# Moving two pieces of work in a fused attention and feed-forward kernel: half of the first output weights ahead of one batch's values, and one batch's row sums into consecutive units

## The chip, the cores and the metric

The kernel runs on one core of a Trainium2 chip. The metric is the device time of one execution in microseconds (us), as a median over several executions. A profile is one execution recorded by the hardware profiler. Its "span" is about 2 us shorter than the time.

The engines are called PE (tensor engine, matmuls), PEld (its weight loads), DVE (VectorE), ACT (ScalarE), POOL (GpSimd) and SP (the engine whose queue issues most transfers here). A "q" behind a name means its sequencer, for example SPq.

## The reference, cut to what matters

```python
# 8 batches, 8 heads, 576 rows, head dimension 64
kv  = einsum('bhsd,bhse->bhde', k, v)          # "states", one 64x64 matrix for each head
o   = einsum('bhsd,bhde->bhse', q, kv)
o   = o / sqrt(mean(o*o, -1) + 1e-6) * g_norm  # row sums of squares are needed here
x   = o.transpose(0, 2, 1, 3).reshape(4608, 512)
xn  = x / sqrt(mean(x*x, -1) + 1e-6) * rms_g
out = (silu(xn @ w_gate) * (xn @ w_val)) @ w_out    # 512 -> 1536 -> 512
```

The inputs and the output are float32. The kernel casts to bf16 for the matmuls.

## The kernel before

It works in nine stages. Stage n runs the feed-forward part for batch n's first 512 rows: twelve "up" units of 8 matmuls each (gate and value, 128 columns of d_ff), then "down" products. Between these units it works on the attention of batch n+1, so that the next stage's input `xnt` is ready in time. The ninth stage does the 64 rows left of every batch.

Stage 0 is special: while it runs, the weights and the inputs of batches 1 and 2 are still coming in. Here are the parts that the change touches.

```python
    # order of loads on SP's queue
    alloc_kv(1, "k"); load_kv(1, "k", nc.sync)
    alloc_kv(1, "v"); load_kv(1, "v", nc.sync)
    load_wo(0)                    # output weights, block 0: two loads of 512 KB
    load_q(1); load_wo(1); load_wo(2); load_batch(2)
    ...
    for j in range(4, NF):        # stage 0's up units 4 to 11
        ffn.up(j)
        ...
        if j == 9:
            for i in range(3): cast_kv(1, "k", i, DVE)
        if j == 10:
            cast_kv(1, "k", 3, DVE)
            for i, engine in enumerate((SC, DVE, GP, DVE)): cast_kv(1, "v", i, engine)
    for i, engine in enumerate((SC, GP, DVE, SC)): round_wo(0, i, 1, engine)
    ...
    att1.kv_products((0, 1, 2, 3))          # states of batch 1: 72 small matmuls
    att1.kv_copy()                          # ACT, then DVE
    clear_tail_rows(1, DVE)                 # two memsets
    for i, engine in enumerate((DVE, SC, DVE, SC)):
        cast_q(1, slice(2 * i, 2 * i + 2), engine)
    for c in range(4):
        down_part(c, 0, 4)                  # 16 down matmuls
    turns.q_turn(0, SC)                     # query transposes on PE; need all four casts
    turns.q_turn(1, DVE)
    for blk in (1, 2):
        for i in range(4): round_wo(blk, i, 1, GP)
    for c in range(2): down_part(c, 4, 6)   # needs the first half of block 1
```

In the later stages a table of steps says after which unit each piece of the next batch's attention runs. `a.o(c)` makes 128 rows of attention output. `a.sums(c)` is a multiplication and a reduction on VectorE. `a.head`, `a.guess` and `a.root` turn the sums into row scales, `a.scale` applies them, and `a.x_rows` transposes the rows by DMA into the next stage's `xnt`.

```python
            kv0, os = (2, (4, 5, 7, 8)) if n == 1 else (0, (2, 3, 5, 6))
            for c, u in enumerate(os):
                steps[u].append(lambda a=a, c=c: a.o(c))
                steps[u + 1].append(lambda a=a, c=c: a.sums(c))
            late = 2 * int(n == 1)
            steps[8 + late] += [a.head]
            steps[9 + late] += [a.guess, a.root]
            ...                             # scale and x_rows in unit 11
```

Of the kernel before, what the change touches and what calls it, by code (L numbers as in the profile page):

```python
# [20 lines left out]
def kernel(  # L21
# [12 lines left out]
    nc = tc.nc  # L34

    B, H, S, D = q.shape
    d_model = H * D
# [40 lines left out]
    PE, DVE, SC, GP = nc.tensor, nc.vector, nc.scalar, nc.gpsimd  # L78
# [20 lines left out]
    wo_view = moe_w_out.rearrange("(c p) d -> p c d", p=128)  # L99

    def stage(n=2048):
        return stage_pool.tile([128, MAIN * T + MAIN], FP32, name="st")[:, 0:n]

    def cast(engine, dst, src):
        if engine is SC:
            engine.copy(out=dst, in_=src)  # L106
        else:
            engine.tensor_copy(out=dst, in_=src)
# [7 lines left out]
    def alloc_kv(b, name):  # L116
        raws[b, name] = stage(MAIN * T + MAIN)

    def pairs_raw(b, name):
        return raws[b, name][:, 0 : NS * C * D].rearrange("p (j x) -> p j x", j=NS)  # L120

    def pairs_buf(b, name):
        flat = bufs[b][name].rearrange("p t h d -> p (t h d)")
        return flat[:, 0 : NS * C * D].rearrange("p (j c d) -> p j c d", j=NS, c=C)

    def load_kv(b, name, queue, js=slice(0, NS)):
        src = srcs[name][b]
        if b < EARLY:
            view = src.rearrange("h s d -> (h s d)").rearrange("(j p x) -> p j x", j=NS, p=128)
            queue.dma_start(out=pairs_raw(b, name)[:, js, :], in_=view[:, js, :])  # L130
            return
        raw = raws[b, name]
        queue.dma_start(
            out=raw[:, 0 : MAIN * T].rearrange("p (h x) -> p h x", h=H),
            in_=src[:, 0:MAIN, :].rearrange("h (p t) d -> p h (t d)", t=T),
        )
        queue.dma_start(
            out=raw[0:TAIL, MAIN * T :].rearrange("r (h d) -> r h d", h=H),
            in_=src[:, MAIN:S, :].rearrange("h r d -> r h d"),
        )  # L140
# [3 lines left out]
    def cast_kv(b, name, i, engine):  # L144

        if b < EARLY:
            cast(engine, pairs_buf(b, name)[:, i].rearrange("p c d -> p (c d)"), pairs_raw(b, name)[:, i, :])
        elif i < NS:
            hs = slice(2 * i, 2 * i + 2)
            src = raws[b, name][:, 0 : MAIN * T].rearrange("p (h t d) -> p t h d", h=H, t=T)  # L150
            cast(engine, bufs[b][name][:, 0:T, hs, :], src[:, :, hs, :])
        else:
            src = raws[b, name][0:TAIL, MAIN * T :].rearrange("r (h d) -> r h d", h=H)
            cast(engine, bufs[b][name][0:TAIL, T], src)

    def load_q(b):
        st = stage()
        raws[b, "q"] = st
        for hs in (slice(0, 4), slice(4, 8)) if b < EARLY else (slice(0, H),):
            nc.sync.dma_start(  # L160
                out=st.rearrange("p (h x) -> p h x", h=H)[:, hs],
                in_=q[b, hs, 0:MAIN, :].rearrange("h (p t) d -> p h (t d)", t=T),
            )
# [4 lines left out]
    def cast_q(b, hs, engine):  # L168
        src = raws[b, "q"].rearrange("p (h t d) -> p t h d", h=H, t=T)[:, :, hs, :]
        cast(engine, bufs[b]["q"][:, :, hs, :], src)  # L170
# [9 lines left out]
    w_st = {}  # L180
# [24 lines left out]
                out=dst, in0=src, scalar1=rowscale[:, s : s + 1], scalar2=1.0, op0=OP.mult, op1=OP.mult  # L205
            )

    def load_wo(blk):
        st = stage()
        ap = st.rearrange("p (c d) -> p c d", d=d_model)  # L210
        for i in (0, 2):
            nc.sync.dma_start(out=ap[:, i : i + 2, :], in_=wo_view[:, 4 * blk + i : 4 * blk + i + 2, :])
        w_st["o", blk] = ap

    def round_wo(blk, i, n, engine):
        c = 4 * blk + i
        cast(engine, wo_sb[:, c : c + n, :], w_st["o", blk][:, i : i + n, :])
# [60 lines left out]
    def clear_tail_rows(i, engine):  # L278

        for t in (kbs[i], vbs[i]):  # L280
            engine.memset(t[TAIL:128, T], 0.0)
# [306 lines left out]
    for j in (2, 3):  # L588
# [4 lines left out]
        out=gam[NS : NS + 1, :].rearrange("o (i d) -> o i d", i=2),  # L593
        in_=g_norm.rearrange("(o d) -> o d", o=1).unsqueeze(1).to_broadcast([1, 2, D]),
# [54 lines left out]
    def state0(j, dummies):  # L649
        ps = att_pool.tile([128, 512], FP32, name="att_ps")  # L650
        warm(ps, max(dummies, 1), 512 if dummies else 128)
        kv_pair(ps[:, 0:128], 0, j, True, True)
        return ps
# [35 lines left out]
    for j in (0, 1):  # L689
        cast_kv(0, "k", j, DVE)  # L690
        cast_kv(0, "v", j, SC)
    kv0 = state0(0, 0)
# [26 lines left out]
        out=gsq, in0=gcol, scalar=1.0 / d_model, in1=gcol, op0=OP.mult, op1=OP.mult  # L719
# [63 lines left out]
            load_w(blk, name, nc.sync)  # L783
    alloc_kv(1, "k")
    load_kv(1, "k", nc.sync)
    alloc_kv(1, "v")
    load_kv(1, "v", nc.sync)
    load_wo(0)
    load_q(1)
    load_wo(1)  # L790
    load_wo(2)
# [44 lines left out]
    for j in range(4, NF):  # L836
        ffn.up(j)
        for s in {4: (0, 1), 5: (2,), 6: (3,)}.get(j, ()):
            round_w(4, "g", s, SC)
        if j == 6:  # L840
            for s in (0, 1):
                round_w(4, "v", s, DVE)
        if j == 7:
            clear_tail_rows(0, DVE)
        if j == 9:
            for i in range(3):
                cast_kv(1, "k", i, DVE)
        if j == 10:
            cast_kv(1, "k", 3, DVE)
            for i, engine in enumerate((SC, DVE, GP, DVE)):  # L850
                cast_kv(1, "v", i, engine)
    for i, engine in enumerate((SC, GP, DVE, SC)):
        round_wo(0, i, 1, engine)
    alloc_xnt(1)

    def f_cols(j):
# [19 lines left out]
    def down_part(c, lo, hi):  # L876
        ffn.down_products(c, lo, hi, pools[c])

    def round_wo_halves(blk):
        round_wo(blk, 0, 2, DVE)  # L880
        round_wo(blk, 2, 2, SC)

    att1.kv_products((0, 1, 2, 3))
    att1.kv_copy()
    clear_tail_rows(1, DVE)
    for i, engine in enumerate((DVE, SC, DVE, SC)):
        cast_q(1, slice(2 * i, 2 * i + 2), engine)
    for c in range(4):
        down_part(c, 0, 4)
    turns.q_turn(0, SC)  # L890
    turns.q_turn(1, DVE)
    for blk in (1, 2):
# [65 lines left out]
    for n in range(1, B + 1):  # L958
        ffn = Ffn(n)
        steps = {u: [] for u in range(NF + T)}  # L960
        if n + 2 < B:
            steps[2].append(lambda n=n: load_batch(n + 2))
        if n == B - 3:
            load_q_tails()
        if n == 1:
            steps[0] += [lambda i=i: cast_kv(2, "k", i, DVE) for i in (2, 3)]
            steps[0] += [lambda i=i: cast_kv(2, "v", i, SC) for i in (0, 1)]
            steps[1] += [lambda i=i: cast_kv(2, "v", i, SC) for i in (2, 3)]
            steps[0] += [lambda name=name: cast_kv(2, name, NS, GP) for name in ("k", "v")]
        if n < B:  # L970
            a = atts[n + 1]
            kv0, os = (2, (4, 5, 7, 8)) if n == 1 else (0, (2, 3, 5, 6))
            if not a.tail:
                steps[kv0] += [lambda a=a: a.kv_products((0, 1))]
                steps[kv0 + 1] += [lambda a=a: a.kv_products((2, 3)), a.kv_copy]
# [6 lines that stand above are left out]
            for c in range(T):  # L982
                steps[10 if c == 0 and not late else 11] += [lambda a=a, c=c: a.scale(c), lambda a=a, c=c: a.x_rows(c)]
        b = n + 2
        if b < B:
            steps[10] += [lambda b=b: alloc_q(b)]
            for i in range(2):
                steps[11] += [lambda b=b, i=i: cast_q(b, slice(4 * i, 4 * i + 4), SC)]
            for i in KV_CASTS:
                steps[12 + i // 3] += [lambda b=b, i=i: cast_kv(b, "k", i, SC)]  # L990
                steps[14 + i // 3] += [lambda b=b, i=i: cast_kv(b, "v", i, SC)]
            for c in range(T):
                steps[13].append(lambda b=b, c=c: atts[b].q_rows(c))
        if b == B:
            for i in range(2):
                steps[11] += [lambda i=i: cast_q_tails(2 * i, 2, SC)]
            for c in range(T):
                steps[13].append(lambda c=c: turn_q_tails(c))
        for unit in range(NF + T):
            if unit < NF:  # L1000
                ffn.up(unit)
            elif n == B and unit == NF + T - 1:
                ffn.down_last(unit - NF)
            else:
                ffn.down(unit - NF)
            for step in steps[unit]:
                step()
# [30 lines left out]
```

## Time and profile before

| | |
|---|---|
| time, median of the first 3 executions | 325.81 us (325.27 to 326.08) |
| span of the profile | 323.0 us |
| PE busy | 315.8 us, 98% |

The first part of the profile page gives the busy time of each engine, its share of the span and its number of instructions. The fourth part gives the shares of the chain that ended last. Here are the two lines of the kernel before.

```profile
PE 315.8 (98%) x1927; PEld 157.1 (49%) x1927; DVE 180.6 (56%) x373; ACT 179.3 (56%) x320; POOL 18.1 (6%) x40
...
PE 88%; DVE 5%; DMA 3%; SPq 2%; issue 1%; ACT 1%; DVEq 0%
```

PE is the bound, so a change can only win where PE stands still. The waits view (who waited for whom: us in total, times, longest) names two of these places in the part that the change touches.

```profile
PE g_ps L473 <- DMA xnt<-xna: 0.5, 1, 0.5
PE att_ps L266 <- DVE vb L108: 0.2, 1, 0.2
```

The second one in the timeline (start, length, engine, line, operation, tiles, count, and in brackets the idle time before): PE runs 18 of batch 1's state products, then stands until VectorE has cast a piece of v. From one start to the next, less the usual pitch, the hole is 0.36 us.

```profile
39.36 0.47 PE L266 MATMUL att_ps<-vb,kb 64*64 64x64 bf16 x18
39.52 0.81 DVE L108 CAST vb<-st 128x576 bf16<-128x576 f32 x2
40.02 1.04 PE L266 MATMUL att_ps<-vb,kb 64*64 64x64 bf16 x54 [0.19 <-DVE vb L108]
```

The first one is at the start of stage 2. In the chain of waits (start, length, what), the last transposed input lands at 89.40 us and PE follows.

```profile
86.80 2.60 DMA xnt<-xna
89.40 0.14 issue
89.54 1.02 PE g_ps L473 x4
```

The last down matmul of stage 1 starts at 88.68 us and takes 0.216 us of PE's pitch. The hole up to 89.54 us is therefore 0.65 us. VectorE's timeline shows where the lateness comes from: the last reduction (L362) ends at 77.86 us, so the `h` product of unit 10 (the second line) and all that follows it are late. The scaling (L379), which feeds the transposes, starts at 81.68 us.

```profile
76.64 1.22 DVE L362 TENSOR_REDUCE ssq<-sq 128x16 f32<-128x1024 bf16 x1
77.78 0.68 DVE L479 TENSOR_TENSOR h_sb<-silu,v_ps 128x512 bf16<-128x512 bf16 x1
78.37 0.17 DVE L366 TENSOR_SCALAR u<-ssq 128x32 f32<-128x32 f32 x1
...
81.68 2.50 DVE L379 TENSOR_TENSOR xna<-outa,s1y 128x512 bf16<-128x512 bf16 x4
```

### The profile page before, as it was taken

To read this page: it belongs to the slowest core of one execution; us is meant where nothing else is said; L and a number is where in the kernel's file an instruction comes from. 1 tells how busy PE (TensorE), PEld (TensorE's weight loads), DVE (VectorE), ACT (ScalarE), POOL (GpSimd) and SP (SyncE) were. 2 spreads that over 40 slices of the span, in tenths; PEclk is the share of its full clock that TensorE was granted. 3 is DMA by queue.
4 is the path that set the end of the run, shared out by engine and by line. 5 is a ranking of instruction groups with operands and counts; after the bars stand their busy time and mean duration, and the time that the engine had idled before them with its cause. 6 is when DMAs were issued, how large, how long until landed. Compare 5 with 4: busy or idle time off the path is not lost.

```text
span 323.0 us, 5146 instructions
## 1 busy us (share of the span) xinstructions
PE 315.8 (98%) x1927; PEld 157.1 (49%) x1927; DVE 180.6 (56%) x373; ACT 179.3 (56%) x320; POOL 18.1 (6%) x40
## 2 busy tenths in 40 slices
PE   8899999999999999999999999999999999999995
PEld 3584455544455445444544455445544444444443
DVE  4785858478437932794279416850696068703310
ACT  3687557666757476647674766576554355233321
POOL 1263241100000000000000000000000000000000
PEclk9999999999999999999999999999999999999999
DMA  7999999996369457934791378946002600240014
GB/s 273 350 349 387 378 373 291 223 282 158 66 196 294 130 137 171 287 91 106 198 335 45 72 202 200 313 79 177 34 2 49 179 34 1 48 148 3 0 35 97
DMA packets 74437, 54.87 MB, mean 170 GB/s; under 512 B 42280, under 2 KB 67116, under 8 KB 74412
## 3 DMA queue, kind: packets, MB, share of 16 engines
q1 hardware_dynamic: 74044, 53.89, 58.2%
q10 hardware_dynamic: 368, 0.66, 0.6%
q8 instruction: 15, 0.25, 0.3%
q14 instruction: 10, 0.08, 0.1%
HBM read 37.75 MB, written 9.44 MB: 146 GB/s over the span
## 4 chain that ended last, share of the span: by engine, by line
PE 88%; DVE 5%; DMA 3%; SPq 2%; issue 1%; ACT 1%; DVEq 0%
PE g_ps L473 27%; PE v_ps L473 26%; PE o_ps L515 23%; PE att_ps L273 2%; DMA st<-in_v_dram 2%; PE att_ps L344 2%; DVE h_sb L479 1%; PE v_ps L490 1%; DMA xnt<-xna 1%; PE v_ps L515 1%; PE g_ps L515 1%; DVE xna L379 1%; DMA out_dram<-o_sb 1%; SPq L386 1%; PE att_ps L266 1%
## 5 line engine op out<-in xcount | busy, mean ns | idle before, releaser
L479 DVE TENSOR_TENSOR h_sb<-silu,v_ps 128x512 bf16<-128x512 bf16 x104 | 70.9, 683 | 110.8 <-ACT silu L478 61.8
L473 PE MATMUL g_ps<-xnt,wg_sb 128*128 128x512 bf16 x416 | 106.8, 379 | 0.5 <-DMA xnt<-xna 0.5
L473 PE MATMUL v_ps<-xnt,wv_sb 128*128 128x512 bf16 x416 | 106.8, 379 | 0.0
L478 ACT ACTIVATE silu<-g_ps 128x512 bf16<-128x512 f32 x104 | 62.4, 601 | 63.9 <-PE g_ps L473 53.7
L515 PE MATMUL o_ps<-wo_sb,h_sb 128*128 128x512 bf16 x396 | 87.4, 379 | 0.0
L473 PEld LDWEIGHTS <-wv_sb 128*128 128x128 bf16 x416 | 40.6, 98 | 49.2 <-DVE wv_sb L204 0.5
L515 PEld LDWEIGHTS <-h_sb 128*128 128x128 bf16 x420 | 40.7, 98 | 47.7
L473 PEld LDWEIGHTS <-wg_sb 128*128 128x128 bf16 x416 | 38.7, 98 | 40.6 <-issue 0.9
L106 ACT COPY o_sb<-o_ps 128x512 f32<-128x512 f32 (+1 forms) x34 | 19.7, 580 | 38.0 <-PE o_ps L515 37.2
L362 DVE TENSOR_REDUCE ssq<-sq 128x16 f32<-128x1024 bf16 x28 | 34.2, 1220 | 1.0
L353 ACT ACTIVATE sq<-att_ps 128x512 bf16<-128x512 f32 x28 | 16.7, 597 | 13.1 <-PE att_ps L344 8.4
L106 ACT CAST vb<-st 128x512 bf16<-128x512 f32 (+2 forms) x33 | 18.9, 625 | 6.0 <-DMA st<-in_v_dram 6.0
L379 DVE TENSOR_TENSOR xna<-outa,s1y 128x512 bf16<-128x512 bf16 x28 | 17.9, 684 | 0.0
L106 ACT CAST qb<-st 128x1024 bf16<-128x1024 f32 (+1 forms) x17 | 15.4, 944 | 2.0 <-DMA st<-in_q_dram 1.8
L355 ACT CAST outa<-att_ps 128x512 bf16<-128x512 f32 x28 | 16.2, 580 | 0.0
L106 ACT CAST kb<-st 128x512 bf16<-128x512 f32 (+1 forms) x25 | 14.0, 619 | 0.0
L361 DVE TENSOR_TENSOR sq<-sq,gsq 128x512 bf16<-128x512 bf16 x28 | 11.7, 418 | 0.0
L344 PEld LDWEIGHTS <-qt 128*128 128x128 bf16 x96 | 7.4, 98 | 5.7
L616 PE MATMUL att_ps<-kv_all 128*128 128x512 bf16 (+1 forms) x23 | 8.2, 480 | 1.2 <-DVE sel L605 1.2
L344 PE MATMUL att_ps<-kv_all,qt 128*128 128x128 bf16 x96 | 9.3, 219 | 0.0
L273 PEld LDWEIGHTS <-kb 128*128 128x128 bf16 x120 | 7.7, 98 | 2.8
L273 PE MATMUL att_ps<-vb,kb 128*128 128x128 bf16 x120 | 8.7, 219 | 0.0
(141 smaller groups left out, 164.3 us busy)
## 6 DMA issues: line engine op xcount, KB each, us to landing
out_dram<-o_sb SPq DMA_DIRECT2D x14, 512.0 KB, 3.0
st<-in_q_dram SPq DMA_DIRECT2D x6, 1024.0 KB, 6.6
st<-in_k_dram SPq DMA_DIRECT2D x6, 1024.0 KB, 9.2
st<-in_v_dram SPq DMA_DIRECT2D x6, 1024.0 KB, 11.3
st<-in_moe_w_out_dram SPq DMA_DIRECT2D x6, 512.0 KB, 10.0
st<-in_moe_w_gate_dram SPq DMA_DIRECT2D x4, 512.0 KB, 7.3
st<-in_moe_w_val_dram SPq DMA_DIRECT2D x4, 512.0 KB, 8.2
st<-in_k_dram SPq DMA_DIRECT2D x4, 288.0 KB, 5.3
```

What stands on the lines that cost most here:

```text
L106: engine.copy(out=dst, in_=src)
L273: PE.matmul(ps, lhsT=bufs[b]["k"][:, t, hs, :], rhs=bufs[b]["v"][:, t, hs, :], start=(first and t == 0), stop=(last and t == T),)
L344: PE.matmul(cols, lhsT=self.qt[:, j, 128 * c : 128 * c + 128], rhs=kv_all[:, self.n, j, :], start=(j == 0), stop=(j == NS - 1),)
L353: SC.activation(out=self.sq[c][:, 0], in_=ps, func=ACT.Square)
L355: SC.copy(out=self.outa[c], in_=ps)
L361: DVE.tensor_tensor(out=sq[:, 1], in0=sq[:, 0], in1=gsq8, op=OP.mult)
L362: DVE.reduce_sum(out=self.ssq[:, c], in_=sq, axis=AX.X)
L379: DVE.tensor_tensor(out=self.xna[c], in0=self.outa[c], in1=self.alpha[:, c, :].to_broadcast([128, H, D]), op=OP.mult)
L473: PE.matmul(ps, lhsT=wt[:, s, j * 128 : (j + 1) * 128], rhs=x[:, s, :], start=(s == 0), stop=(s == NS - 1),)
L478: SC.activation(out=silu, in_=g_ps, func=ACT.Silu)
L479: DVE.tensor_tensor(out=self.h[:, j, :], in0=silu, in1=v_ps, op=OP.mult)
L515: PE.matmul(self.o_ps[c], lhsT=self.h[:, j, c * 128 : (c + 1) * 128], rhs=wo_sb[:, j, :], start=(j == 0), stop=(j == NF - 1),)
```

## The change

The intent is twofold. In stage 0, PE gets eight down matmuls to do (chunks 0 and 1 of all four row blocks) before it needs batch 1's v. For that, the first half of the output weights must arrive before v. In stage 1, batch 2's sums lie in consecutive units, so that VectorE is done with them one unit earlier.

```diff
     load_kv(1, "k", nc.sync)
+    load_wo(0, (0,))
     alloc_kv(1, "v")
     load_kv(1, "v", nc.sync)
-    load_wo(0)
+    load_wo(0, (2,))
 ...
+        if j == 8:
+            for i in range(2):
+                cast_kv(1, "k", i, DVE)
+                round_wo(0, i, 1, GP)
         if j == 9:
-            for i in range(3):
-                cast_kv(1, "k", i, DVE)
+            cast_kv(1, "k", 2, DVE)
         if j == 10:
             cast_kv(1, "k", 3, DVE)
-            for i, engine in enumerate((SC, DVE, GP, DVE)):
-                cast_kv(1, "v", i, engine)
-    for i, engine in enumerate((SC, GP, DVE, SC)):
-        round_wo(0, i, 1, engine)
+    for i, engine in enumerate((SC, DVE, GP, SC)):
+        cast_kv(1, "v", i, engine)
+    for i in (2, 3):
+        round_wo(0, i, 1, GP)
 ...
+    for c in range(4):
+        down_part(c, 0, 2)
     att1.kv_products((0, 1, 2, 3))
+    for i, engine in enumerate((DVE, SC)):
+        cast_q(1, slice(2 * i, 2 * i + 2), engine)
     att1.kv_copy()
     clear_tail_rows(1, DVE)
-    for i, engine in enumerate((DVE, SC, DVE, SC)):
-        cast_q(1, slice(2 * i, 2 * i + 2), engine)
+    for i, engine in enumerate((DVE, SC)):
+        cast_q(1, slice(2 * i + 4, 2 * i + 6), engine)
     for c in range(4):
-        down_part(c, 0, 4)
+        down_part(c, 2, 4)
 ...
-            kv0, os = (2, (4, 5, 7, 8)) if n == 1 else (0, (2, 3, 5, 6))
+            kv0, os = (2, (4, 5, 6, 7)) if n == 1 else (0, (2, 3, 5, 6))
```

`load_wo` also gets an argument that says which halves to load. That is left out here.

## The prediction

> **What bounds it now.** The tensor engine: the page's first part shows PE busy 315.8 of 323.0 us (98%); the chain of waits is 88% PE. Matmuls of 512 columns start every 0.216 us; in the timeline, starts further apart than that show these holes after the preamble:
> - 0.36 us at 39.7 us: batch 1's state products (k times v) wait for VectorE's cast of v (waits view: 0.19 us), plus 0.1 us at each switch between 64-row and 128-row matmuls.
> - 0.08 us at 46.2 us: wait for VectorE's copy of qt.
> - 0.10 us at 61.4 us: unit 3 of stage 1 waits for a silu that sits on ScalarE behind casts of batch 2's v, landed at about 59.8 us.
> - 0.65 us at 88.7 us: stage 2 waits for its last transposed input (waits view: 0.48 us on the xnt transfer).
>
> Transfers run at 350 to 390 GB/s from 8 to 52 us (windows view): near the ~435 GB/s that the Trainium skill, "Perfetto Trace Analysis", Roofline, gives for the 16 engines.
>
> **What the change does.** No matmul is added or removed; instructions move.
> 1. Half of the first out weights (512 KB, about 1.33 us of landing) lands before batch 1's v, which lands at about 38.6 instead of 37.3 us. Eight down matmuls (1.73 us) go before the state products, which then start at about 41.1 us; the v casts should be done by 40.6. The 0.36 us hole closes. GpSimd now casts all four pieces (0.61 us each); while it runs, VectorE's 576-column casts take 0.74 instead of about 0.41 us (the skill's "GPSIMD Engine Reference" names SBUF interfaces shared with VectorE; the trace agrees). There is room for it.
> 2. Most of that 0.36 us is lost at once. State copies, two clears (0.27 us each) and a query cast now form a chain on VectorE after the products, until about 44.35 us, so the query transposes start 0.1 us earlier, not 0.36. Then GpSimd's cast of the second piece of out-weight block 1 ends at 45.52 us, set by a transfer whose place in the queue is unchanged. Then batch 2's v, also unchanged in the queue, holds ScalarE until about 61.5 us. I expect 0 to 0.1 us left by then.
> 3. Batch 2's sums move from units 5, 6, 8, 9 to 5 to 8. VectorE needs 0.68 + 0.42 + 1.22 = 2.3 us in such a unit against PE's 1.95 us, so h products slip by up to 1 us, but the v_ps buffers leave about 0.5 us to spare: no PE wait. Unit 10 no longer waits for the last reduction, which ended at 77.86; head, root and scaling start about 0.65 us earlier, the four transposes with them (82.4 becomes 81.8), and the hole at 88.7 us shrinks from 0.65 to 0.0 to 0.1 us.
>
> **On the critical path:** about 0.6 us from step 3, 0.05 from steps 1 and 2. Later stages are unchanged.
>
> **Predicted: 325.15 us**, 8 in 10 within 324.5 to 325.8. Chances: faster by over 2% 0.01, within 2% 0.98, slower by over 2% 0.01.
>
> **Right or wrong in the profile:** PE's wait on xnt at 88.7 us falls under 0.15 us; its wait for v's cast is gone; waits for GpSimd's wo_sb or VectorE's qb appear at 44 to 46 us; units 1 to 3 of stage 1 end where batch 2's v lets them (61.5 us).
>
> **What would make it wrong:** batch 2's v landing 0.3 us sooner or later; the state products waiting for v after all; late h products stalling v_ps in units 8 to 11; transposes paced by something other than the scaling.

## The result, and the profile after

The median of the changed kernel is 325.14 us (323.88 to 325.66, 6 executions). The kernel before had 325.39 us (325.15 to 326.08, 6 executions). The ratio is 0.9981, with a 95% interval of 0.9958 to 1.0003. A ratio here is the mean time of one kernel's fast executions over that of the other's in the same rounds, so it is not quite the ratio of the medians that are quoted. Executions over 1.5% slower than the fastest of the same kernel are left out of the means. The interval includes 1: the times alone do not show a gain.

The profile of the changed kernel even has a longer span, 323.5 us against 323.0 us. To see why, cut the span at events that every profile has. U is the first weight load of stage 0's unit 4, S of stage 1's unit 0, D of stage 1's down products, N of stage 2's unit 0. The table is worked out from the starts in the traces, in us.

| profile | U | U to S | S to D | D to N | N to end |
|---|---|---|---|---|---|
| before | 25.38 | 30.11 | 22.83 | 11.19 | 233.53 |
| after | 26.44 | 30.29 | 22.74 | 10.54 | 233.53 |

Three things happened. The start, whose code the change does not touch, took 1.06 us longer. Stage 0 from U on lost 0.18 us. Stage 1 won 0.09 + 0.65 us. The 0.09 us is the hold at 61.4 us that the prediction lists, and it cannot be put down to the change: the second profile of the kernel before (e2 below) does not have it either.

The win is as planned. VectorE's four reductions now lie one behind the other. The last one ends at 77.75 us, the head starts at 78.86 us (L367), and the scaling at 82.17 us (L380). With the start taken out, that is 0.66 us sooner: from D to the scaling it took 3.36 us before and takes 2.70 us after.

```profile
76.53 1.22 DVE L363 TENSOR_REDUCE ssq<-sq 128x16 f32<-128x1024 bf16 x1
77.66 1.27 DVE L480 TENSOR_TENSOR h_sb<-silu,v_ps 128x512 bf16<-128x512 bf16 x2
78.86 0.17 DVE L367 TENSOR_SCALAR u<-ssq 128x32 f32<-128x32 f32 x1
...
82.17 2.50 DVE L380 TENSOR_TENSOR xna<-outa,s1y 128x512 bf16<-128x512 bf16 x4
```

In the chain of waits at the start of stage 2 the transfer is gone: down products are followed by up products without a hole.

```profile
84.43 5.78 PE o_ps L516 x26
90.20 0.86 PE g_ps L474 x4
```

The loss is in the chain of waits of the changed kernel between 43 and 47 us. Read it downwards: the state products end, ACT and then VectorE copy the states, VectorE clears the tail rows of k and v (L282), then it casts a piece of q. Only then do the query transposes (L827) go on.

```profile
43.00 0.43 PE att_ps L267 x26
43.43 0.02 issue
43.45 0.38 ACT kv_all L310
43.83 0.02 issue
43.85 0.43 DVE kv_all L311
44.28 0.00 issue
44.28 0.27 DVE kb L282
44.55 0.00 issue
44.56 0.27 DVE vb L282
44.83 0.03 issue
44.86 0.90 DVE qb L108
45.76 0.05 issue
45.80 0.95 PE att_ps L827 x14
```

The cast takes 0.89 us. The 512-column cast of q that VectorE did at 42.01 us took 0.43 us. GpSimd is casting output weights in the same moment:

```profile
44.85 2.52 POOL L108 CAST wo_sb<-st 128x512 bf16<-128x512 f32 x4 [3.16 <-DMA st<-in_moe_w_out_dram]
```

Before the change both of VectorE's query casts together took 0.88 us and were over before GpSimd began, and the sixteen transposes ran through:

```profile
42.50 0.88 DVE L108 CAST qb<-st 128x512 bf16<-128x512 f32 x2
...
44.34 1.18 POOL L108 CAST wo_sb<-st 128x512 bf16<-128x512 f32 x2 [5.05 <-DMA st<-in_moe_w_out_dram]
44.46 1.06 PE L825 MATMUL att_ps<-identity,qb 128*128 128x128 bf16 x16
```

The waits view of the changed kernel lists the new wait, and the wait for VectorE's cast of v is gone from it:

```profile
PE att_ps L827 <- DVE qb L108: 0.4, 1, 0.4
```

The hole inside the query transposes, from start to start less the pitch, is 0.61 us. The one it replaces was 0.36 us.

### The profile page after: what moved, and what is told of

Same layout as the page of the kernel before. It is cut to its first block, busy times and chain, and to the rows that moved or that the text cites. A ratio compares the mean times of both kernels' runs of the same rounds, so it can differ in the third digit from the quotient of the medians.

```text
span 323.5 us, 5112 instructions
## 1 busy us (share of the span) xinstructions
PE 313.6 (97%) x1893; PEld 157.0 (49%) x1927; DVE 181.2 (56%) x371; ACT 178.9 (55%) x319; POOL 20.9 (6%) x43
## 4 chain that ended last, share of the span: by engine, by line
PE 86%; DMA 6%; DVE 4%; issue 2%; ACT 1%; DVEq 0%
PE v_ps L474 26%; PE o_ps L516 26%; PE g_ps L474 26%; DMA st<-in_k_dram 3%; DMA st<-in_moe_w_gate_dram 3%; PE att_ps L274 2%; PE att_ps L345 2%; DVE h_sb L480 1%; DVE ssq L363 1%; PE v_ps L516 1%; PE g_ps L516 1%; DMA out_dram<-o_sb 1%; PE o_ps L491 1%; PE att_ps L340 0%; ACT wg_sb L202 0%
## 5 line engine op out<-in xcount | busy, mean ns | idle before, releaser
L474 PE MATMUL v_ps<-xnt,wv_sb 128*128 128x512 bf16 x409 | 105.7, 379 | 0.4
L474 PE MATMUL g_ps<-xnt,wg_sb 128*128 128x512 bf16 x401 | 104.9, 379 | 0.8 <-ACT wg_sb L202 0.2
L380 DVE TENSOR_TENSOR xna<-outa,s1y 128x512 bf16<-128x512 bf16 x28 | 17.9, 684 | 0.0
```

Source lines behind the costliest of these rows:

```text
L380: DVE.tensor_tensor(out=self.xna[c], in0=self.outa[c], in1=self.alpha[:, c, :].to_broadcast([128, H, D]), op=OP.mult)
L474: PE.matmul(ps, lhsT=wt[:, s, j * 128 : (j + 1) * 128], rhs=x[:, s, :], start=(s == 0), stop=(s == NS - 1),)
```

## The experiments

The main theory: the gain is the sums' alone (0.65 us, D to N). The order part of the change costs a few tenths, because VectorE's clears and a collision with GpSimd hold the query transposes longer than v held the state products. The rest of the difference between two times is chance in the start (U). The rivals: the change itself delays the start; the two parts need each other; or, as I had predicted, the place of the transfers bounds stage 0, so that removing VectorE's delay would win nothing.

### 1 and 2. Both kernels once more

There is no edit. These two runs ask what chance alone does.

> The changed kernel once more, for more times and a second profile. Intervals between the first weight loads of: stage 0's unit 4 (U), stage 1's unit 0 (S), stage 1's down products (D), stage 2's unit 0 (N). Theory: the later start of the changed kernel's profile (U at 26.44 us against 25.38) is chance in the load of the first inputs, so U differs here (anywhere in 25.3 to 26.6), while S-U stays 30.2 to 30.4, D-S 22.7 to 22.9, N-D 10.5 to 10.6. Rival: the change itself delays the start, then U is again 26.3 to 26.6. Ratio to the kernel before 0.996 to 1.000.

> The kernel before against itself: what chance alone does to a ratio and to U. Theory (start is chance): ratio 0.998 to 1.002, U anywhere in 25.3 to 26.6, with S-U 30.1, D-S 22.8, N-D 11.2 as in its first profile. Rival (the change delays the start): U again within 0.2 us of 25.38.

Measured: the changed kernel has 325.01 us (6 executions) and a ratio of 0.9990 (0.9968 to 1.0013). The kernel before, against itself, has a ratio of 0.9997 (0.9982 to 1.0013).

| profile | U | U to S | S to D | D to N |
|---|---|---|---|---|
| e1, changed kernel | 25.68 | 30.28 | 22.73 | 10.52 |
| e2, kernel before | 25.91 | 29.76 | 22.74 | 11.10 |

U is now earlier in the changed kernel than in the kernel before. So the late start of the first profile does not come from the change.

There was also a miss. U to S of the kernel before is 29.76 us, not 30.1. The hole at the state products is 0.07 us here and not 0.36. PE came to them half a microsecond later, and v's casts were nearly done. In the three fast profiles with this order (before, e2, and e3 below) the hole is the smaller, the later PE starts: 0.36, 0.07 and 0 us at U 25.38, 25.91 and 27.45 us.

### 3 and 4. Each half of the change alone

```diff
 # e3, on the kernel before
-            kv0, os = (2, (4, 5, 7, 8)) if n == 1 else (0, (2, 3, 5, 6))
+            kv0, os = (2, (4, 5, 6, 7)) if n == 1 else (0, (2, 3, 5, 6))
 # e4, on the changed kernel
-            kv0, os = (2, (4, 5, 6, 7)) if n == 1 else (0, (2, 3, 5, 6))
+            kv0, os = (2, (4, 5, 7, 8)) if n == 1 else (0, (2, 3, 5, 6))
```

> Only the sums of batch 2 move to consecutive units; loads and order of stage 0 as before. Theory: the sums are the whole gain: N-D falls from 11.2 to 10.5 us, S-U stays 30.1, D-S 22.8; 0.6 us faster than before (ratio 0.998), and 0.1 to 0.2 us faster than the changed kernel. Rival (the gain needs the order change too, because the held silu bounds stage 1): N-D falls, but D-S grows by as much.

> Only the load and order part of the change; sums of batch 2 as before. Theory: S-U grows by 0.1 to 0.2 us (30.3) because the query cast behind the two clears holds the query transposes longer than the state products waited before; N-D stays 11.2; ratio 1.000 to 1.001. Rival (my prediction, a small gain from closing the 0.36 us hole): S-U 30.0 to 30.1.

| profile | U | U to S | S to D | D to N | median, ratio to before |
|---|---|---|---|---|---|
| e3, sums only | 27.45 | 29.68 | 22.73 | 10.55 | 325.04, 0.9986 (0.9968 to 1.0003) |
| e4, order only | 27.41 | 30.00 | 22.73 | 11.17 | 325.92, 1.0011 (0.9992 to 1.0030) |

The gain in D to N follows the sums, and S to D does not pay for it. The order part alone has a larger U to S than the kernel before's order has at the same late start (30.00 against 29.68 us). The holes say the same: in e4 the query transposes stand for 0.31 us, and in e3 there is none.

Three expectations missed. In e3, U to S was to stay at 30.1 us and is 29.68 us, since at this late start there was no hole to close. Its median is 325.04 us, not 0.1 to 0.2 us below the changed kernel's (325.01 us in e1). In e4, U to S was to be 30.3 us and is 30.00 us, which is the figure of its rival. So that figure alone cannot decide between the two, and the comparison at the same start has to.

In e3, with the old order, GpSimd's casts did fall on VectorE's two query casts, which took 0.76 and 0.83 us. PE lost nothing by it, because its sixteen down matmuls lasted until 46.1 us and the casts ended at 45.7 us.

Both profiles started late, and the windows view (stretch, then busy time of each engine, granted clock, transfers) shows one reason. In e3 the granted clock (the column behind POOL) falls to 0.64 on average between 12 and 16 us. It does not in the profile of before, which comes second:

```profile
12.00:16.00 4.00, 3.90 (x44) 2.08 (x43) 1.80 (x10) 1.98 (x5) 2.19 (x5) 0.64 1.09 361
...
12.00:16.00 4.00, 3.68 (x41) 2.23 (x41) 2.61 (x10) 2.56 (x7) 1.86 (x4) 1.00 1.06 351
```

In the trace's clock record it is one period of 3.41 us at half clock, in both e3 and e4. The Trainium skill, "TensorE: Matmul & The Clock Gate", Part 1, describes such a gate with a window of 3413 ns, and the length agrees. PE had been busy for 2.17 us (e3) and 2.27 us (e4) of the four microseconds from 8 to 12 us. It had been busy for 2.51 to 3.14 us of that stretch in all ten fast profiles without the drop. That this sets off the drop is argued, not shown, and the stretch was chosen afterwards: the least busy 3.41 us between 5 and 22 us is 51% busy in e3 and e4, but in e8 and e12 as well, which kept the full clock. Nor is the drop the only reason for a late U: e5 and e11 below have 26.89 and 26.95 us without it.

### 5. Clears out of the way (run e5)

```diff
     att1.kv_copy()
-    clear_tail_rows(1, DVE)
 ...
     ffn.down_out(1)
     alloc_q(2)
     cast_q(2, slice(0, 4), SC)
     down_part(2, 8, 12)
+    clear_tail_rows(1, DVE)
     f_x(2, xs[2], DVE)
```

> The changed kernel with the two clears of batch 1's tail rows moved from before the third query cast to the slot where VectorE later waits for the transposed rows. Theory (the clears push VectorE's query cast behind, and into GpSimd's casts of the next out weights): that cast starts 0.54 us earlier after the state products, takes about 0.45 instead of 0.88 us, the query transposes run without the 0.61 us hole, S-U falls from 30.28 to 29.7 us. Rival (a transfer bounds this stretch, as predicted: out-weight block 1 and GpSimd's cast of it): the hole moves behind the transposes to the down products of chunk 4 and 5, S-U stays above 30.0.

Measured: U 26.89, U to S 29.67, S to D 22.73, D to N 10.52 us. The median is 324.65 us (4 executions), the ratio 0.9974 (0.9953 to 0.9995). The chain of waits over the stretch that held the long VectorE chain is now PE alone:

```profile
43.86 0.97 PE o_ps L516 x4
44.83 0.43 PE g_ps L516 x2
45.26 0.43 PE v_ps L516 x2
45.69 0.89 PE att_ps L827 x16
46.59 0.22 PE o_ps L516
```

VectorE's cast starts directly after the state copy, takes 0.43 us, and is over before GpSimd begins:

```profile
44.76 0.43 DVE L108 CAST qb<-st 128x512 bf16<-128x512 f32 x1
45.31 1.17 POOL L108 CAST wo_sb<-st 128x512 bf16<-128x512 f32 x2 [3.17 <-DMA st<-in_moe_w_out_dram]
```

The first line is from VectorE's timeline, the second from GpSimd's. U to S fell by the whole 0.61 us. The rival, my own prediction's step that a transfer would bound this stretch, is refuted here: nothing moved behind the transposes. The four profiles without the clears in the way (e5, e7, e9, e11) have U at 26.09 us or later, so a start as early as 25.38 us is not tested.

### 6. The collision alone (run e8)

```diff
+    for i in range(2):
+        round_wo(1, i, 1, SC)
     turns.q_turn(0, SC)
     turns.q_turn(1, DVE)
     for blk in (1, 2):
         for i in range(4):
-            round_wo(blk, i, 1, GP)
+            if (blk, i) not in ((1, 0), (1, 1)):
+                round_wo(blk, i, 1, GP)
```

> The changed kernel with the casts of the first half of out-weight block 1 on ScalarE instead of GpSimd; the clears stay. Theory (contention of GpSimd and VectorE makes up 0.4 us of the 0.61 us hole, the clears' place the rest): the third query cast takes 0.45 us instead of 0.88, the hole inside the query transposes falls to 0.1 to 0.25 us, S-U to 29.8 to 30.0 us. Rival (contention plays no part): the cast still takes over 0.8 us and the hole stays 0.6.

Measured: U 25.74, U to S 29.88, S to D 22.73, D to N 10.50 us. The median is 324.66 us (4 executions), the ratio 0.9977 (0.9961 to 0.9992). The clears are still there, GpSimd is not, and the cast is short:

```profile
43.59 0.27 DVE L282 MEMSET kb<- 64x256 uint32 x1
43.86 0.27 DVE L282 MEMSET vb<- 64x256 uint32 x1
44.16 0.43 DVE L108 CAST qb<-st 128x512 bf16<-128x512 f32 x1
```

The hole inside the query transposes is 0.15 us. So of the 0.61 us the collision makes up 0.46 us and the clears the rest. The Trainium skill, "GPSIMD Engine Reference", Specifications, says that GpSimd's SBUF interfaces are shared with VectorE, with contention for certain kinds of VectorE instructions. The trace agrees for these casts and gives the size: 0.46 us on a cast of 0.43 us.

### 7. A mended version, and two more kernels

The mended version, e7, adds to e5 that batch 2's first two v casts come behind unit 1's silu on ScalarE. In the first profile of the kernel before, that silu had held PE for 0.10 us at 61.4 us, behind casts that waited for batch 2's v.

```diff
-            steps[0] += [lambda i=i: cast_kv(2, "v", i, SC) for i in (0, 1)]
+            steps[1] += [lambda i=i: cast_kv(2, "v", i, SC) for i in (0, 1)]
```

> Clears moved as in the run before, and the first two casts of batch 2's v put behind unit 1's silu on ScalarE instead of ahead of it. Theory: S-U 29.7, and D-S 22.7 whatever U is, since the silu no longer waits for batch 2's v; against the changed kernel 0.6 us gained in S-U, ratio to the kernel before 0.996 to 0.998. Rival (late v casts stall batch 2's state products instead): D-S grows to 23 or more when U is early.

Measured: U 26.09, U to S 29.68, S to D 22.83, D to N 10.51 us. The median is 324.44 us, the ratio 0.9968 (0.9956 to 0.9981). Whether the silu's place matters stays open. S to D was 22.73 or 22.74 us in all other fast profiles but the very first, so the hold that this edit removes came in one profile only. The extra 0.1 us in e7 itself is a hole between the weights and the first matmul of stage 1's first unit.

e9 adds to e7 that the two small loads of the norm weights go early on ScalarE's queue, right behind its two loads of batch 0's v:

```diff
+    nc.scalar.dma_start(out=gam[0:NS, :], ...)
+    nc.scalar.dma_start(out=gam[NS : NS + 1, :]..., ...)
     SC.preload_act_table(ACT.Sqrt)
 ...
-    nc.sync.dma_start(out=gam[0:NS, :], ...)
-    nc.sync.dma_start(out=gam[NS : NS + 1, :]..., ...)
```

> As the run before, and the two small loads of the norm weights issued first on ScalarE's queue, instead of behind six loads on the other. Theory (the start varies because the tensor engine waits 0.35 to 0.94 us for these loads at 11 us, and in two of six profiles the clock was then granted at half for 3.4 us): the wait for gam is gone, U comes at 25.0 to 25.6 us with a full clock, spread of the times smaller; 321.8 to 322.3 us span, ratio to before 0.993 to 0.996. Rival (the start is bound by batch 0's v and q landing, gam only stands in the same queue): U stays 25.4 to 26.5 with other waits, ratio as the run before.

Measured: 324.29 us (324.02 to 324.66), ratio 0.9961 (0.9948 to 0.9975). The wait for gam is gone, but U is 26.39 us. PE waited at nearly the same place for the cast of batch 0's v instead, in the waits view:

```profile
PE att_ps L267 <- ACT vb L106: 1.4, 1, 1.4
```

So in this profile the rival was right about U: without the wait for gam, PE waited for batch 0's v instead. The six times spread less than those of the other kernels with six fast times. One set of six does not show that this is the edit's doing.

Last, the mended version and the changed kernel once more on the same chip, beside e10. That is the kernel before with only the sums and the silu edit.

> The kernel before with the sums of batch 2 in consecutive units and the silu of unit 1 ahead of the v casts, but without the load and order part. Theory (the order part, mended, gains only where the start is early, by at most the 0.36 us hole): S-U 29.7 when U is 26 or later and up to 30.1 when U is near 25.4; ratio to before 0.997 to 0.9985, within 0.3 us of the mended version. Rival (the order part is worth its 0.36 us in most runs): at least 0.4 us slower than the mended version.

> The mended version (clears late, silu first) once more, beside the changed kernel on the same chip: S-U 29.7, D-S 22.7 to 22.8, N-D 10.5; 0.5 to 0.7 us faster than the changed kernel; ratio to before 0.996 to 0.998.

> The changed kernel a third time: S-U 30.3, D-S 22.7, N-D 10.5 whatever U is; ratio to before 0.997 to 1.000.

| kernel | median | ratio to before | U | U to S | D to N |
|---|---|---|---|---|---|
| e10, sums and silu edit, no order part | 324.28 (4 of 5 fast) | 0.9968 (0.9954 to 0.9981) | slow profile | | |
| e11, mended | 324.59 | 0.9980 (0.9962 to 0.9997) | 26.95 | 29.68 | 10.52 |
| e12, changed kernel | 324.62 | 0.9985 (0.9969 to 1.0001) | 25.66 | 29.84 | 10.54 |

The profile of e10 fell in a slow execution (granted clock 0.95 throughout, 337.19 us), and is not used. Its four fast times are no slower than the mended version's. So the rival there, that the order part is worth 0.36 us in most runs, finds no support. e11 missed its expected 0.5 to 0.7 us over the changed kernel: the medians are 0.03 us apart. Part of the reason is e12's own miss. U to S was 29.84 us and not 30.3, since the hole inside the query transposes was 0.15 us. In e12 VectorE's cast began 0.01 us before GpSimd's, and it was GpSimd that was held:

```profile
44.08 0.43 DVE L108 CAST qb<-st 128x512 bf16<-128x512 f32 x1
...
44.09 1.45 POOL L108 CAST wo_sb<-st 128x512 bf16<-128x512 f32 x2 [3.16 <-DMA st<-in_moe_w_out_dram]
```

The first of these two GpSimd casts took 0.89 us instead of the usual 0.61, and VectorE's took its usual 0.43 us. In the first profile of the changed kernel GpSimd began 0.01 us ahead and took 0.62 us, and VectorE's took 0.89 us. So the changed kernel's cost here depends on which of two casts begins first, and GpSimd's begins when a transfer lands. The five fast profiles that have both the new order and the clears in place agree: the cast took 0.89, 0.88, 0.59, 0.43 and 0.43 us (after, e1, e4, e8, e12), and the hole was 0.61, 0.60, 0.31, 0.15 and 0.15 us, always 0.28 us less.

Taken over all its executions, the changed kernel has a mean of 324.92 us (18 executions, 323.88 to 326.43). The mended version has 324.55 us (12 executions, 323.74 to 325.55). The kernel before has 325.45 us (45 executions, 324.71 to 326.37). These come from several rounds, so they are a summary and not a test. That the mended version beats the kernel before is shown twice by intervals (0.9968 and 0.9980, both below 1). That it beats the changed kernel is shown by the profile's intervals (U to S 29.68 against 29.84 to 30.29 us), not by times.

## Why the prediction was right or wrong, point by point

The predicted time was 325.15 us, and the measured median was 325.14 us. Part of that agreement is luck. The predicted effect, 0.65 us, is about as large as what the start alone does: U differs by 0.53 us between the first two profiles of the kernel before, and by 0.76 us between those of the changed kernel. And it was taken off a base of 325.81 us, the median of three executions; over six the kernel before has 325.39 us, so the two medians lie only 0.25 us apart.

- **Step 3, the sums: right in mechanism and size.** Predicted: scaling 0.65 us sooner, the hole at stage 2 from 0.65 to at most 0.1 us, no wait for v_ps in units 8 to 11. Measured: 0.66 us sooner, D to N 11.19 to 10.54 us, no such wait, and D to N of 10.50 to 10.55 us in eight profiles with the edit (10.36 in e9, where stage 2's first weights were loaded sooner and N to the end grew by as much).
- **Step 1, the state products: right for that profile.** The wait for v's cast is gone. What I had not seen is that the hole was this large in a profile that started early (U 25.38). At U 25.91 it was 0.07 us, and in e3, at U 27.45, it was nil.
- **Step 2, the transition: the step that failed.** "I expect 0 to 0.1 us left by then" was a small gain. The first two profiles show a loss of 0.18 us (U to S 30.11 to 30.29). Against the second profile of before it is 0.5 us. The chain that I named (state copies, clears, query cast) is the right one. The mis-sized term is the query cast. I took it as about 0.44 us after the clears, and it took 0.89 us, because it fell on GpSimd's casts of the next output weights. I had used this very collision in step 1, for other casts, and did not ask where GpSimd would be at 44.9 us. The wait itself was on my list of signs ("VectorE's qb" at 44 to 46 us), but not its length. The two bounds that I named behind it did not bind. Without the clears in the way (e5), the transposes ran through and nothing waited for block 1. Batch 2's v did not hold stage 1 in the changed kernel's profile either: PE came 1.2 us later, and unit 3 started at 62.7 us. In e12 stage 1 began as early as in the first profile (55.50 us), and there was no hold either: ScalarE's cast of that v began at 59.19 us, against 59.86 us.
- **The sum.** Averaged over the fast profiles, D to N fell from 11.15 (before, e2, e4) to 10.54 us (after, e1, e3, e12), a gain of 0.62 us. U to S rose from 29.85 (before, e2, e3, which share the order before) to 30.10 us (after, e1, e4, e12, which share the changed order), a loss of 0.25 us. The net is about 0.4 us. The three ratios of the changed kernel (0.9981, 0.9990, 0.9985) stand for 0.3 to 0.6 us. What the order part does on average rests on few profiles with different starts, and it is the less certain number.
- **Left out altogether: the start.** U lay between 25.38 and 27.45 us in the twelve fast profiles. The range of 324.5 to 325.8 us was wide enough for the median, but single executions lay outside it on both sides.

## What to carry to other kernels

Before pulling work ahead to fill a hole, look at what the engines that feed the next step do in the new order: here a 0.36 us hole was traded for one of up to 0.61 us, because two memsets and a cast slid into the moment when GpSimd was casting too. When the effect is smaller than the scatter of the times, cut each profile at events that all kernels share and compare the pieces: D to N agreed within 0.05 us in eight profiles of kernels whose times scattered by over 2 us. And a hole seen in one profile may belong to that execution's start, so look at a second profile before building on it.

## What the Trainium skill lacked or had wrong

- "GPSIMD Engine Reference", Specifications, names the shared SBUF interfaces, but gives no size there. Who waits is said elsewhere in the skill, so only the figures are added here. A 0.43 us VectorE cast took 0.89 us when GpSimd's began 0.01 us earlier. When VectorE's began 0.01 us earlier, it kept its 0.43 us, and GpSimd's took 0.89 instead of 0.61 us.
- "TensorEngine Tiling (Array Packing)", Key Properties, says that changing the tiling mode drains the engine, but gives no cost. Here a switch between 64-row and 128-row matmuls left a hole of 0.09 to 0.10 us in most places, and of 0.07 us at the least.
- "TensorE: Matmul & The Clock Gate", Part 1, names an idle window as what drops the clock, and in a further case frequent short idle times, without a share. Here the clock fell to half for 3.41 us after four microseconds in which PE was busy 54 to 57% of the time and never stood still for more than 0.94 us (e3, e4). It did not fall after 63 to 79% in the ten other fast profiles, one of which (e9) had a standstill of 1.44 us.
- No page says how much the start of a kernel can scatter: with the same code, a fixed event in the first 30 us came between 25.38 and 27.45 us.
